# Projecting queries as plain float32 products, and normalising a pair of heads in one product

## The chip, the cores and the metric

One core of a Trainium2 chip runs the whole kernel in one launch. The metric is the device time of an execution in microseconds (us). The kernel before has a median of 1037.31 us over 3 runs (1033.46 to 1041.04).

The engines that matter here: TensorE (PE in the profile, with its weight loads as PEld) does matrix products into PSUM; VectorE (DVE) and ScalarE (ACT) work elementwise on SBUF and PSUM; GpSimd (POOL) works elementwise on SBUF; SyncE (SP) issues all of this kernel's DMAs, one after the other. Each engine executes its instructions in the order in which they were given to it.

## The reference

```python
def phi(x):                                   # x: (4, 8, 576, 64)
    proj = np.einsum('bhsd,df->bhsf', x, w_phi)        # 128 features
    proj = proj - np.max(np.abs(proj), axis=-1, keepdims=True)
    return np.concatenate([np.exp(proj), np.exp(-proj)], axis=-1)
q_p, k_p = (phi(q), phi(k))
kv  = np.einsum('bhsf,bhsd->bhfd', k_p, v)
z   = np.sum(k_p, axis=2)
num = np.einsum('bhsf,bhfd->bhsd', q_p, kv)
den = np.einsum('bhsf,bhf->bhs', q_p, z)[..., None] + 1e-06
x   = (num / den)                             # -> (2304 tokens, 512)
x   = (h * np.cos(h)) @ w_out                 # h = x @ w_in, hidden 2048
out = (np.maximum(h2, 0) + alpha * np.minimum(h2, 0)) @ w_out2   # h2 = x @ w_in2
```

The weights of the two layers arrive as 64-bit floats and are decoded on the chip.

## The kernel before

**Number formats.** TensorE is given two kinds of operand: float32, and float32r, a float32 with a shortened fraction. To keep precision with float32r, a value is split into a high part `hi` (a cast to float32r) and a low part `lo` (the value less `hi`), and a product is made of three: hi·hi, hi·lo, lo·hi. The keys, the queries, `w_phi`, the numerators' operands and both layers are split like this; products of keys' features and values (`kv`) and the transposes of the queries are float32.

**Attention.** The 32 heads are 8 groups of four; a group is two pairs of two heads. The tokens of a group are cut into five chunks: four chunks of two tiles (a tile is 128 rows that hold 128 tokens of both heads of a pair, 256 columns of features), and one chunk of one tile with the last 64 tokens of both pairs. There are 40 chunks of keys and 40 of queries. The loop over `s` (line 710) is the step: in step `s` chunk `s` of the keys is projected and chunk `s - 2` of the queries. The tuple `order` (line 667) lists the stages of a step by hand, and that order is the order on every engine (`tc.manual_schedule()`, line 61).

The queries' way: `load_x` (SP, L358), `split_hi` (DVE cast, L436), `split_lo` (DVE subtraction, L443), `project` (PE, three products per tile, L455) into one of three PSUM buffers `pj` that keys and queries share, `maximum` (DVE, L467), `less_max` (DVE, L475), `q_transpose` (PE, L536), `q_exp` (ACT L555 and L569, then POOL L571 for the low part), `num` (PE, L580), `num_out` (ACT, L593). The keys' way is the same to `less_max`, with the cast on ACT and the subtraction on POOL; then `k_exp` (ACT, L484) and `kv` (PE, L496). Of `kv`, a head's product has 66 columns (64 values, ones, zeros); in the one-tile chunk it has 132.

**Normalising a pair.** When a pair's numerators have left PSUM, `num_out` issues a DMA of the denominators into a tile `dn` (L596). One step later `recip` adds EPS and takes the reciprocal on DVE (L601, L602), writes it to DRAM (L604) and reads it back twice, each head's 576 values broadcast to 64 partitions (L606). One step after that `x_mult` (DVE, L612) multiplies head by head, partitions 0 to 63; the second head's result is written to partitions 64 to 127. Then `x_split` (ACT L621, POOL L623) makes the layers' input `xh`, `xl`.

**Decoding weights.** A part of the weights is ten instructions (`w_instructions`, line 93). Four parts are decoded during the attention, one begun every ten steps (`W_AT`); with `spare=True` DVE does the cast to the high part (L114) and the last subtraction and addition (L132, L133), which in the later parts ACT and POOL do.

**The layers.** From step `S_H` the first products of the layers (L161) run beside the end of the attention, and then alone: 160 steps of hidden product, gate and output product.

Of the kernel before, what the change touches and what calls it, by code (L numbers as in the profile page):

```python
# [23 lines left out]
WARM = 9                    # products that raise the tensor engine's clock  # L24
# [4 lines left out]
def feature_map_attention_two_mlps(  # L29
# [17 lines left out]
    NG4 = qT.shape[0]       # groups of four heads  # L47
# [102 lines left out]
    # ---- the two layers, in steps: a 128-wide part of the hidden dimension for a group of  # L150
    # tokens, and the products that read the part of LEAD steps before
# [91 lines left out]
    # Blocks of parts of the hidden dimension; the first ones are small, so that few weights  # L243
    # have to be on chip when the attention ends. Short group of tokens away from the ends.
# [14 lines left out]
    # A part of the weights is decoded when the last reader of its place has been issued and  # L259
    # before its own first reader is, the rest of the time evenly.  # L260
# [58 lines left out]
    # ---- attention  # L319
    # Group n holds four heads of a batch: two pairs pr of two heads y. A tile has 128 rows  # L320
    # (tokens) for both heads of a pair; the last tile holds the last 64 tokens of both pairs.
    with ExitStack() as actx:
# [23 lines left out]
        xin, xs_h, xs_t, pjs, mxs, tt, kp, kvs = ({} for _ in range(8))  # L346
        q_ps, qp, nm_ps, nums, dens = ({} for _ in range(5))
        kv_todo = []
        rb = (acc[3][0:D, 2 * S:3 * S], acc[4][0:D, 0:S])

        def load_x(kind, i):
            n, c = divmod(i, NC)
            w = len(chunks[c]) * P
            if n == 0:
                return
            t = pool_of[kind].tile([P, 2 * P], F32, tag=f"{kind}in", name=f"{kind}in")
            src = qT if kind == "q" else kT
            nc.sync.dma_start(out=t[:, :w], in_=src[n, :, first[c] * P:first[c] * P + w])  # L358
            xin[kind, i] = t
# [22 lines left out]
        wraw = acc[4][:, S:S + F]  # L382
# [4 lines left out]
        def load_first(kind, c, to):  # L387
            # chunks of the first group, into places that the attention needs later
# [6 lines left out]

        load_first("k", 0, 1)
        for j in range(2):
            nc.sync.dma_start(out=wraw[j * D:(j + 1) * D, :], in_=w_phi)
        load_first("k", 1, 3)
        # the tensor engine's clock is raised while the first inputs arrive  # L400
# [5 lines left out]
        # the exponential's table is loaded while the first inputs arrive  # L406
# [3 lines left out]
        nc.vector.memset(w2h.bitcast(F32), 0.0)  # L410
        nc.vector.memset(w2l.bitcast(F32), 0.0)
# [10 lines left out]
        make_identity(nc, ident)  # L422
        def w_phi_split():
            for j in range(2):
                r = slice(j * D, (j + 1) * D)
                (nc.vector.tensor_copy if j == 0 else nc.scalar.copy)(w2h[r, j, :], wraw[r, :])
                nc.vector.tensor_tensor(
                    out=w2l[r, j, :], in0=wraw[r, :], in1=w2h[r, j, :].bitcast(F32), op=ALU.subtract
                )

        # ---- the stages: i is a chunk, n a group, pr a pair
        def split_hi(kind, i):
            w = len(chunks[i % NC]) * P
            t = xin.pop((kind, i))
            hi = pool_of[kind].tile([P, 2 * P], F32R, tag=f"{kind}h", name=f"{kind}h")
            (nc.scalar.copy if kind == "k" else nc.vector.tensor_copy)(hi[:, :w], t[:, :w])  # L436
            xs_h[kind, i] = (t, hi)

        def split_lo(kind, i):
            w = len(chunks[i % NC]) * P  # L440
            t, hi = xs_h.pop((kind, i))
            lo = pool_of[kind].tile([P, 2 * P], F32R, tag=f"{kind}l", name=f"{kind}l")
            (nc.gpsimd if kind == "k" and i > 1 else nc.vector).tensor_tensor(  # L443
                out=lo[:, :w], in0=t[:, :w], in1=hi[:, :w].bitcast(F32), op=ALU.subtract
            )
            xs_t[kind, i] = (hi, lo)

        def project(kind, i):
            nt = len(chunks[i % NC])
            hi, lo = xs_t.pop((kind, i))  # L450
            pj = ps_pj.tile([P, 2, 2, F], F32, tag="pj", name="pj")
            for a in range(nt):
                s = slice(a * P, (a + 1) * P)
                for m, (l, r) in enumerate(((hi, w2h), (hi, w2l), (lo, w2h))):
                    nc.tensor.matmul(  # L455
                        pj[:, a].rearrange("p j f -> p (j f)"),
                        lhsT=l[:, s],
                        rhs=r.rearrange("p j f -> p (j f)"),
                        start=(m == 0),
                        stop=(m == 2),  # L460
# [78 lines left out]
        def q_exp(i, s, lo):  # L539
# [4 lines left out]
            # columns of tp: tile a, head y (last tile: head y, pair x); parts as (pair, half  # L544
            # of the pair's columns, columns)
# [53 lines left out]
        def recip(n, pr):  # L599
            dn = dens.pop((n, pr))  # L600
            nc.vector.tensor_scalar(out=dn, in0=dn, scalar1=EPS, scalar2=None, op0=ALU.add)  # L601
# [206 lines left out]
```

## Time and profile before

| | |
|---|---|
| runs | 1033.46, 1037.31, 1041.04 us |
| span of the profiled execution, first to last instruction | 1038.0 us (the page gives no other time for it) |
| PE busy | 996.6 us, 96% |
| DVE busy | 755.5 us, 73% |
| ACT busy | 505.3 us, 49% |
| POOL busy | 635.5 us, 61% |
| chain that ended last, by engine | PE 73%, DVE 15%, POOL 4%, issue 3% |
| mean granted TensorE clock | 0.990 of full speed |

A busy share is a mean over the whole span. The attention (about the first 213 us) and the layers (the rest) load the engines differently, so that the shares say little until they are read stretch by stretch. "Busy" is the time in which at least one instruction of an engine was under way. Durations of matmuls in the trace contain their latency; what one costs in a row of them is read from the distance of their starts. Of the rows by line, the number behind the last bar is the idle time of the engine just before such an instruction, with what ended it.

### The profile page before, as it was taken

The numbers are of one execution on the slowest core, as the hardware profiler recorded it, in microseconds if no ns is written. First come the engines' busy times: TensorE is split into PE (matmuls) and PEld (weight loads), VectorE is DVE, ScalarE is ACT, GpSimd is POOL, SyncE is SP. The second block draws the span as 40 slices with busy tenths as digits, with TensorE's granted clock in tenths as the row PEclk, the third lists the DMA queues.
The fourth block names the chain that finished last, engine by engine and source line by source line (L and its number), as shares of the span: only waits on it lengthen the run. The fifth ranks groups of instructions, "written<-read, shape, count | busy, mean of one in ns | idle before, by whom it ended". The sixth has DMA issues, their size and how long they took to land.

```text
span 1038.0 us, 14530 instructions
## 1 busy us (share of the span) xinstructions
PE 996.6 (96%) x5289; PEld 846.4 (82%) x5289; DVE 755.5 (73%) x1090; ACT 505.3 (49%) x1004; POOL 635.5 (61%) x528
## 2 busy tenths in 40 slices
PE   8988888889999999999999999799999999999998
PEld 7888888877888888888888888688888888888887
DVE  6999999976887747765775678567756874777433
ACT  5878777776666556564656573213222231232100
POOL 3878778675666636663657589737564665566411
PEclk8999999999999999999999999999999999999999
DMA  4543433211111101110111011101110111111112
GB/s 119 132 109 96 107 94 96 60 45 51 43 61 46 57 20 42 61 41 22 61 41 41 21 61 41 41 21 62 41 41 23 59 42 40 41 42 41 41 41 102
DMA packets 63303, 58.31 MB, mean 56 GB/s; under 512 B 28672, under 2 KB 54400, under 8 KB 63232
## 3 DMA queue, kind: packets, MB, share of 16 engines
q1 hardware_dynamic: 63232, 57.38, 18.7%
q8 instruction: 42, 0.69, 0.3%
q14 instruction: 29, 0.24, 0.1%
HBM read 52.50 MB, written 4.79 MB: 55 GB/s over the span
## 4 chain that ended last, share of the span: by engine, by line
PE 73%; DVE 15%; POOL 4%; issue 3%; ACT 2%; DMA 1%; SPq 0%; DVEq 0%; POOLq 0%; ACTq 0%
PE po L161 35%; PE ph L161 33%; DVE acc L612 3%; DVE acc L475 3%; PE kv L496 2%; PE nm L580 2%; DVE mx L467 2%; PE pj L455 2%; POOL xl L86 2%; DVE ql L443 1%; DVE we L118 1%; DVE qh L436 1%; DVE wt L122 1%; POOL gl L86 1%; DVE wt L125 1%
## 5 line engine op out<-in xcount | busy, mean ns | idle before, releaser
L86 POOL TENSOR_TENSOR gl<-r,gh 128x512 fp32r<-128x512 f32 (+1 forms) x160 | 201.8, 1263 | 323.7 <-ACT gh L85 314.7
L85 ACT CAST gh<-r 128x512 fp32r<-128x512 f32 (+1 forms) x160 | 92.1, 575 | 387.3 <-DVE r L207 262.1
L161 PE MATMUL ph<-xh,wih 128*128 128x512 f32 (+1 forms) x640 | 237.1, 371 | 2.2 <-DVE kvl L527 2.2
L161 PE MATMUL ph<-xh,wil 128*128 128x512 f32 (+1 forms) x640 | 237.3, 371 | 0.0
L161 PE MATMUL ph<-xl,wih 128*128 128x512 f32 (+1 forms) x640 | 236.5, 370 | 0.0
L236 DVE TENSOR_TENSOR acc<-po,acc 128x512 f32<-128x512 f32 (+1 forms) x134 | 87.0, 659 | 103.8 <-PE po L161 103.3
L161 PEld LDWEIGHTS ph<-xh,wih 128*128 128x128 f32 x640 | 120.8, 189 | 24.5 <-DVE kvl L527 2.5
L161 PEld LDWEIGHTS ph<-xl,wih 128*128 128x128 f32 x640 | 120.8, 189 | 22.3
L161 PEld LDWEIGHTS ph<-xh,wil 128*128 128x128 f32 x640 | 120.9, 189 | 21.4
L161 PE MATMUL po<-gh,woh 128*128 128x512 f32 (+1 forms) x320 | 119.0, 372 | 2.3 <-DVE acc L234 2.3
L161 PE MATMUL po<-wol,gh 128*128 128x512 f32 x288 | 114.8, 399 | 5.3 <-POOL wol L133 5.3
L161 PE MATMUL po<-gh,wol 128*128 128x512 f32 (+1 forms) x320 | 119.6, 374 | 0.1
L161 PE MATMUL po<-gl,woh 128*128 128x512 f32 (+1 forms) x320 | 118.9, 372 | 0.0
L161 PE MATMUL po<-woh,gh 128*128 128x512 f32 x288 | 114.4, 397 | 0.0
L161 PE MATMUL po<-woh,gl 128*128 128x512 f32 x288 | 114.0, 396 | 0.0
L122 DVE SCALAR_TENSOR_TENSOR wt<-ws,we 128x512 int32<-128x512 int32 x64 | 99.8, 1559 | 2.2
L194 DVE TENSOR_SCALAR r<-ph,al 128x512 f32<-128x512 f32 (+1 forms) x80 | 55.3, 691 | 57.3 <-PE ph L161 31.7
L131 POOL TENSOR_TENSOR wu<-wu,we 128x512 f32<-128x512 f32 x64 | 86.0, 1343 | 2.1 <-ACT wu L128 2.1
L571 POOL TENSOR_TENSOR qp1l<-acc,qp1h 128x512 fp32r<-128x512 f32 (+1 forms) x64 | 65.6, 1052 | 28.3 <-ACT qp1h L569 28.1
L205 DVE TENSOR_TENSOR r<-ph,r 128x512 f32<-128x512 f32 (+1 forms) x80 | 50.6, 632 | 43.5 <-ACT r L192 43.4
L496 PE MATMUL kv<-vm,kp 128*128 128x66 f32 x512 | 74.5, 261 | 4.2 <-DVE kvl L527 2.3
L496 PEld LDWEIGHTS kv<-vm,kp 128*128 128x128 f32 x512 | 73.1, 195 | 6.3 <-ACT qp1h L569 2.9
(106 smaller groups left out, 2077.3 us busy)
## 6 DMA issues: line engine op xcount, KB each, us to landing
ws<-in_moe_w_in_dram SPq DMA_DIRECT2D x32, 512.0 KB, 3.7
ws<-in_moe_w_out_dram SPq DMA_DIRECT2D x32, 512.0 KB, 3.5
acc<-dr SPq DMA_DIRECT2D x32, 144.0 KB, 3.3
out_dram<-acc SPq DMA_DIRECT2D x18, 256.0 KB, 2.0
vm<-in_v_dram SPq DMA_DIRECT2D x16, 256.0 KB, 3.6
kin<-in_k_dram SPq DMA_DIRECT2D x28, 128.0 KB, 3.0
qin<-in_q_dram SPq DMA_DIRECT2D x28, 128.0 KB, 2.8
vt<-in_v_dram SPq DMA_DIRECT2D x16, 32.0 KB, 3.4
```

Source lines behind the costliest of these rows:

```text
L85: nc.scalar.copy(hi, src)
L86: lo_engine.tensor_tensor(out=lo, in0=src, in1=hi.bitcast(F32), op=ALU.subtract)
L122: lambda: stt(out=t, in0=w1, scalar=-0x40000000, in1=e, op0=ALU.bitwise_and, op1=ALU.bitwise_or),
L131: lambda: tt(out=u, in0=u, in1=ef, op=ALU.mult),
L161: nc.tensor.matmul(ps, lhsT=l, rhs=r, start=(first and m == 0), stop=(last and m == n - 1))
L194: nc.vector.tensor_scalar(out=r, in0=ph, scalar1=0.0, scalar2=al[:, ft:ft + 1], op0=ALU.min, op1=ALU.mult)
L205: nc.vector.tensor_tensor(out=r, in0=ph, in1=r, op=ALU.mult)
L236: nc.vector.tensor_tensor(out=a, in0=po, in1=a, op=ALU.add)
L475: nc.vector.tensor_tensor(out=t, in0=pj, in1=mx.unsqueeze(2).to_broadcast(list(pj.shape)), op=ALU.subtract)
L496: nc.tensor.matmul(ps[:, :, y, :] if pr is None else ps[:, pr, y, :], lhsT=e[:, s, 2 * a + y, :], rhs=vt[:, y] if pr is None else vm[:, pr ...
L571: nc.gpsimd.tensor_tensor(out=dl, in0=et, in1=dh.bitcast(F32), op=ALU.subtract)
L612: nc.vector.tensor_tensor(out=o[y * D:(y + 1) * D, 0, :], in0=o[0:D, y, :], in1=rb[y], op=ALU.mult)
```

## The change

For the queries `split_hi` and `split_lo` are gone: `project` gives TensorE the loaded float32 tile and a float32 copy `w2` of the weights, one product per tile in place of three. The tile `qin` has four buffers in place of two. `recip` first issues a DMA that copies the second head's numerators from partitions 0 to 63 to partitions 64 to 127, and the broadcasts go to 64 partitions per head of one of two places; `x_mult` is then one multiplication per pair on 128 partitions. The four parts decoded in the attention take `spare=False`. `w2` is cleared before its two DMAs, and `w_phi_split` works on it whole.

```diff
-        rb = (acc[3][0:D, 2 * S:3 * S], acc[4][0:D, 0:S])
+        rb = (acc[3][:, 2 * S:3 * S], acc[4][:, 0:S])
...
-            t = pool_of[kind].tile([P, 2 * P], F32, tag=f"{kind}in", name=f"{kind}in")
+            t = pool_of[kind].tile([P, 2 * P], F32, tag=f"{kind}in", name=f"{kind}in", bufs=4 if kind == "q" else 2)
...
-        wraw = acc[4][:, S:S + F]
+        w2 = const.tile([P, 2, F], F32, name="w2")
...
+        nc.vector.memset(w2, 0.0)
         load_first("k", 0, 1)
         for j in range(2):
-            nc.sync.dma_start(out=wraw[j * D:(j + 1) * D, :], in_=w_phi)
+            nc.sync.dma_start(out=w2[j * D:(j + 1) * D, j, :], in_=w_phi)
...
         def w_phi_split():
-            for j in range(2):
-                r = slice(j * D, (j + 1) * D)
-                (nc.vector.tensor_copy if j == 0 else nc.scalar.copy)(w2h[r, j, :], wraw[r, :])
-                nc.vector.tensor_tensor(
-                    out=w2l[r, j, :], in0=wraw[r, :], in1=w2h[r, j, :].bitcast(F32), op=ALU.subtract
-                )
+            nc.vector.tensor_copy(w2h, w2)
+            nc.vector.tensor_tensor(out=w2l, in0=w2, in1=w2h.bitcast(F32), op=ALU.subtract)
...
         def project(kind, i):
             nt = len(chunks[i % NC])
-            hi, lo = xs_t.pop((kind, i))
+            if kind == "q":
+                x = xin.pop((kind, i))
+                products = ((x, w2),)
+            else:
+                hi, lo = ks_t.pop(i)
+                products = ((hi, w2h), (hi, w2l), (lo, w2h))
...
         def recip(n, pr):
             dn = dens.pop((n, pr))
+            nc.sync.dma_start(out=nums[n, pr][D:2 * D, 0, :], in_=nums[n, pr][0:D, 1, :])
             nc.vector.tensor_scalar(out=dn, in0=dn, scalar1=EPS, scalar2=None, op0=ALU.add)
             nc.vector.reciprocal(dn, dn)
...
                 nc.sync.dma_start(
-                    out=rb[y], in_=dr[y * S:(y + 1) * S].unsqueeze(0).to_broadcast([D, S])
+                    out=rb[pr][y * D:(y + 1) * D, :],
+                    in_=dr[y * S:(y + 1) * S].unsqueeze(0).to_broadcast([D, S]),
                 )
 
-        def x_mult(n, pr, y):
-            o = nums[n, pr]
-            nc.vector.tensor_tensor(
-                out=o[y * D:(y + 1) * D, 0, :], in0=o[0:D, y, :], in1=rb[y], op=ALU.mult
-            )
+        def x_mult(n, pr):
+            x = nums[n, pr][:, 0, :]
+            nc.vector.tensor_tensor(out=x, in0=x, in1=rb[pr], op=ALU.mult)
...
-                w_run.extend(zip((s + d for d in W_PART), w_instructions()))
+                w_run.extend(zip((s + d for d in W_PART), w_instructions(spare=False)))
...
-            chunk(split_hi, 2 - LAG, kind="q"),
...
-            chunk(split_lo, 2 - LAG, kind="q"),
...
-            group(x_mult, after(2), LAG, 0),
-            group(x_mult, after(2), LAG, 1),
+            group(x_mult, after(2), LAG),
```

## Rows read from the trace of the kernel before

**Rows 1.** Windows: stretch in us, its length, each engine's busy time (instructions), granted clock, DMA.

```profile
core 0: us, PE busy (x) PEld busy (x) DVE busy (x) ACT busy (x) POOL busy (x), PEclk, DMA share, GB/s
14.00:213.00 199.00, 174.81 (x1463) 167.28 (x1463) 190.69 (x321) 154.78 (x374) 152.17 (x143) 0.98 0.36 93
67.34:120.48 53.14, 45.29 (x387) 42.91 (x385) 52.09 (x88) 41.59 (x102) 42.50 (x40) 1.00 0.39 101
...
262.00:1038.00 776.00, 766.96 (x3575) 634.42 (x3574) 522.46 (x700) 313.81 (x562) 449.73 (x347) 1.00 0.14 45
```

**Rows 2.** Waits of the engines from 67.34 to 120.48 us: total, times, longest.

```profile
POOL qp1l L571 <- ACT qp1h L569: 7.1, 5, 2.4
...
PE pj L455 <- DVE acc L475: 4.9, 5, 2.5
POOL xl L623 <- ACT xh L621: 4.6, 4, 1.4
...
PE tp L536 <- DVE acc L475: 1.4, 1, 1.4
```

**Rows 3.** Groups by line on DVE, 67.34 to 120.48 us: busy, mean ns, idle before.

```profile
L612 DVE TENSOR_TENSOR acc<-acc,acc 64x576 f32<-64x576 f32 x7 | 9.4, 1339 | 0.1
L443 DVE TENSOR_TENSOR ql<-qin,qh 128x256 fp32r<-128x256 f32 (+1 forms) x10 | 6.7, 672 | 0.0
L436 DVE CAST qh<-qin 128x256 fp32r<-128x256 f32 (+1 forms) x10 | 5.3, 530 | 0.0
...
L133 DVE TENSOR_TENSOR wil<-wt,wu 128x512 fp32r<-128x512 f32 x1 | 1.0, 1035 | 0.1
L114 DVE CAST wih<-wt 128x512 fp32r<-128x512 f32 x1 | 1.0, 961 | 0.0
...
L132 DVE TENSOR_TENSOR wt<-wt,wih 128x512 f32<-128x512 f32 x1 | 0.8, 837 | 0.0
```

**Rows 4.** The line of x_mult: duration ns min/median/max, first and last start.

```profile
L612 DVE TENSOR_TENSOR acc<-acc,acc x27: 737/905/1822, 50.9 to 237.8; 64x576 f32<-64x576 f32 x27
```

**Rows 5.** Timeline of PE, 60 to 90 us: start, us, instruction, how many in a row.

```profile
69.07 0.39 PE L580 MATMUL nm<-qp1l,kvh 128*66 128x320 f32 x1
69.30 0.39 PE L496 MATMUL kv<-vt,kp 128*128 128x132 f32 x2
69.44 0.39 PE L580 MATMUL nm<-qp1h,kvl 128*66 128x320 f32 x1
...
70.40 0.31 PE L580 MATMUL nm<-qp1h,kvl 128*66 128x320 f32 x1
70.55 0.30 PE L580 MATMUL nm<-qp1h,kvh 128*66 128x320 f32 x1
...
72.56 0.28 PE L455 MATMUL pj<-w2h,qh 128*128 128x256 f32 x1
...
72.91 0.28 PE L455 MATMUL pj<-w2h,qh 128*128 128x256 f32 x1
...
73.27 1.90 PE L496 MATMUL kv<-vm,kp 128*128 128x66 f32 x16
75.00 0.39 PE L536 MATMUL tp<-ident,acc 128*128 128x128 f32 x2
```

**Rows 6.** Decoding of the later parts: duration ns min/median/max, first and last start.

```profile
L114 ACT CAST wih<-wt x30: 613/616/622, 245.5 to 920.6; 128x512 fp32r<-128x512 f32 x30
L132 POOL TENSOR_TENSOR wt<-wt,wih x30: 1287/1305/1486, 248.2 to 923.3; 128x512 f32<-128x512 f32 x30
L133 POOL TENSOR_TENSOR wil<-wt,wu x30: 1276/1298/1623, 249.6 to 924.6; 128x512 fp32r<-128x512 f32 x30
```

**Rows 7.** Timeline of DVE, 79 to 89 us: one pair's reciprocal and products.

```profile
79.54 0.16 DVE L601 TENSOR_SCALAR dn<-dn 128x9 f32<-128x9 f32 x1
...
86.61 2.50 DVE L612 TENSOR_TENSOR acc<-acc,acc 64x576 f32<-64x576 f32 x2
```

**Rows 8.** Timeline of SP, 79 to 83 us: the same pair's DMAs.

```profile
79.98 0.33 SPq L604 DMA_DIRECT2D dr<-dn  x1
81.40 1.09 SPq L606 DMA_DIRECT2D acc<-dr  x2
```

**Rows 9.** Page, DMA issues: line, count, KB each, median us from issue to landing.

```profile
acc<-dr SPq DMA_DIRECT2D x32, 144.0 KB, 3.3
```

**Rows 10.** Timeline of PE, 216 to 219 us: where the layers begin, idle before in brackets.

```profile
218.22 0.65 PE L161 MATMUL ph<-xh,wih 128*128 128x512 f32 x1 [2.22 <-DVE kvl L527]
```

More of the change, by code (lines that the diff above doesn't have):

```diff
@@ L345, in feature_map_attention_two_mlps @@
         pool_of = {"q": wk, "k": kw}
-        xin, xs_h, xs_t, pjs, mxs, tt, kp, kvs = ({} for _ in range(8))
+        xin, ks_h, ks_t, pjs, mxs, tt, kp, kvs = ({} for _ in range(8))
         q_ps, qp, nm_ps, nums, dens = ({} for _ in range(5))
         kv_todo = []
-        rb = (acc[3][0:D, 2 * S:3 * S], acc[4][0:D, 0:S])
+        rb = (acc[3][:, 2 * S:3 * S], acc[4][:, 0:S])
         def load_x(kind, i):
@@ L409, in feature_map_attention_two_mlps @@
         nc.vector.memset(half_pi, math.pi / 2)
-        nc.vector.memset(w2h.bitcast(F32), 0.0)
-        nc.vector.memset(w2l.bitcast(F32), 0.0)
         for vm, vt in vbuf:
@@ L423, in w_phi_split @@
         def w_phi_split():
-            for j in range(2):
-                r = slice(j * D, (j + 1) * D)
-                (nc.vector.tensor_copy if j == 0 else nc.scalar.copy)(w2h[r, j, :], wraw[r, :])
-                nc.vector.tensor_tensor(
-                    out=w2l[r, j, :], in0=wraw[r, :], in1=w2h[r, j, :].bitcast(F32), op=ALU.subtract
-                )
-        def split_hi(kind, i):
-            w = len(chunks[i % NC]) * P
[L434 to L437, printed above, removed]
@@ L439, in split_lo, with split_hi @@
-        def split_lo(kind, i):
+            nc.vector.tensor_copy(w2h, w2)
+            nc.vector.tensor_tensor(out=w2l, in0=w2, in1=w2h.bitcast(F32), op=ALU.subtract)
+        def split_hi(i):
+            w = len(chunks[i % NC]) * P
+            t = xin.pop(("k", i))
+            hi = kw.tile([P, 2 * P], F32R, tag="kh", name="kh")
+            nc.scalar.copy(hi[:, :w], t[:, :w])
+            ks_h[i] = (t, hi)
+        def split_lo(i):
             w = len(chunks[i % NC]) * P
-            t, hi = xs_h.pop((kind, i))
-            lo = pool_of[kind].tile([P, 2 * P], F32R, tag=f"{kind}l", name=f"{kind}l")
-            (nc.gpsimd if kind == "k" and i > 1 else nc.vector).tensor_tensor(
+            t, hi = ks_h.pop(i)
+            lo = kw.tile([P, 2 * P], F32R, tag="kl", name="kl")
+            (nc.gpsimd if i > 1 else nc.vector).tensor_tensor(
@@ L444, in split_lo @@
                 out=lo[:, :w], in0=t[:, :w], in1=hi[:, :w].bitcast(F32), op=ALU.subtract
             )
-            xs_t[kind, i] = (hi, lo)
+            ks_t[i] = (hi, lo)
         def project(kind, i):
             nt = len(chunks[i % NC])
-            hi, lo = xs_t.pop((kind, i))
+            if kind == "q":
[4 more added lines that the diff above has]
+                products = ((hi, w2h), (hi, w2l), (lo, w2h))
@@ L451, in project @@
             pj = ps_pj.tile([P, 2, 2, F], F32, tag="pj", name="pj")
             for a in range(nt):
-                s = slice(a * P, (a + 1) * P)
-                for m, (l, r) in enumerate(((hi, w2h), (hi, w2l), (lo, w2h))):
+                for m, (l, r) in enumerate(products):
                     nc.tensor.matmul(
                         pj[:, a].rearrange("p j f -> p (j f)"),
-                        lhsT=l[:, s],
+                        lhsT=l[:, a * P:(a + 1) * P],
                         rhs=r.rearrange("p j f -> p (j f)"),
@@ L459, in project @@
                         start=(m == 0),
-                        stop=(m == 2),
+                        stop=(m == len(products) - 1),
                     )
@@ L654, in go @@
                 i = s + d
-                if 0 <= i < NK and not (f == split_hi and kind == "k" and i < 2):
+                if 0 <= i < NK and not (f == split_hi and i < 2):
                     f(*(() if kind is None else (kind,)), i, *a)
@@ L676, in feature_map_attention_two_mlps @@
             chunk(q_exp, -LAG - 2, 1, False),
-            chunk(split_hi, 2, kind="k"),
+            chunk(split_hi, 2),
             chunk(q_exp, -LAG - 2, 1, True),
@@ L687, in feature_map_attention_two_mlps @@
             group(num, NUM_AT, LAG),
-            chunk(split_lo, 2, kind="k"),
+            chunk(split_lo, 2),
             chunk(maximum, -LAG, kind="q"),
             lambda s: kv_some(),
-            chunk(split_lo, 2 - LAG, kind="q"),
             chunk(q_transpose, -LAG - 1),
             group(kv_lo, KV_AT, 0),
-            group(x_mult, after(2), LAG, 0),
-            group(x_mult, after(2), LAG, 1),
+            group(x_mult, after(2), LAG),
             chunk(less_max, -LAG, kind="q"),
@@ L704, in feature_map_attention_two_mlps @@
         assert S_H < S_O < S_H + LEAD_H
-        split_hi("k", 0)
-        split_lo("k", 0)
+        split_hi(0)
+        split_lo(0)
         w_phi_split()
-        split_hi("k", 1)
-        split_lo("k", 1)
+        split_hi(1)
+        split_lo(1)
         for s in range(NS):
```

## The prediction

> **What bounds the kernel now.** I read the windows first, then who waits for whom, and only then the single groups. The windows [rows 1] show two kernels in one. After 262 us TensorE is busy 767.0 of 776 us: the layers are bound by its products, none of which the change touches, so I carry these 776 us over unchanged. In the attention, 14 to 213 us, the engine that hardly rests is VectorE: 190.7 of 199 us, against 174.8 on TensorE, 154.8 on ScalarE and 152.2 on GpSimd.
>
> The order of stages repeats every ten steps (two groups of heads, one decoded part of the weights). I take one such stretch as a ledger, 67.34 to 120.48 us, 53.14 us long: VectorE 52.1, TensorE 45.3, GpSimd 42.5, ScalarE 41.6 [rows 1]. The waits in it say the same [rows 2]: TensorE's largest are for VectorE's `less_max` (4.9 and 1.4 us of its 53.14 - 45.29 = 7.9 idle). GpSimd's, 7.1 and 4.6 us, are for ScalarE. So VectorE sets the pace, but the others have only 8 to 12 us of room per stretch: relief on VectorE can be worth that much at most, whatever is taken from it. 199 / 53.14 = 3.7 such stretches lie in the attention.
>
> **What leaves VectorE, per stretch.** The queries' splits: 6.7 + 5.3 = 12.0 us [rows 3]. The decoding's cast, subtraction and addition: 1.0 + 0.8 + 1.0 = 2.8 us [rows 3]. Of eight multiplications of a head, four remain, one per pair; seven of them cost 9.4 us, 1.34 each [rows 3], so about 5.4 us go. One multiplication took between 0.74 and 1.82 us [rows 4]; the new one has the same 576 columns on twice the partitions, both ends stand for it too (2.9 to 7.3 us per stretch), and I take the mean. Together 20.2 us: VectorE would have about 32 us of work in a stretch, far from the bound. It is not the gain.
>
> **What is added.** TensorE: a query tile costs three products now, 72.91 - 72.56 = 0.35 us [rows 5]. A float32 product shows as two instructions (the `kv` rows). Nearest to the new one, with more columns than a weight load hides behind, is the 132-column `kv`: from one `nm` to the next with two of them between takes 69.44 - 69.07 = 0.37 us, an `nm` alone 70.55 - 70.40 = 0.15, so the two take 0.22, and for 256 columns I take 0.22 x 256/132 = 0.43 us. That is 0.08 more per tile, and 18 tiles in a stretch make 1.5 us. The bounds: two instructions at the pace of the split ones, 2 x 0.35/3 = 0.23, would save 2.2 us per stretch; at the pace of the 66-column `kv`, sixteen in 75.00 - 73.27 = 1.73 us, thus 0.108 per 66 columns, it is 0.84 us a tile, and 8.8 us more per stretch. I stay at the 132-column row, since the 66-column ones follow each other at a pace that their columns don't explain (half the columns, the same 0.11 us).
>
> The Trainium skill (FP8 and Floating Point Precision, TensorE Precision Notes) counts a true float32 product as four passes through the array, against the three split products here. By that rule a tile would cost a third more than 0.35 us, which is an estimate of 0.47, and the stretch 2.1 us in place of 1.5; the total would come out 2 us later than mine. The `kv` row puts it a little under four, and I keep to the row.
>
> GpSimd gets the subtraction and the addition of a decoded part, 1.31 + 1.30 = 2.6 us per stretch, ScalarE the cast, 0.62 us [rows 6]: GpSimd 45.1, ScalarE 42.2.
>
> The second head's copy: one DMA per pair, ahead of `dr` in SyncE's order. Its issue costs about half of the 1.09 us that two broadcasts take there [rows 8], its landing I put at that of the 144 KB broadcast, 3.3 us [rows 9]; the ends are nothing (it flies while the reciprocal goes out and comes back) and its whole 3.3 us in the pair's chain. The multiplication stands in front of the query's `less_max` on VectorE, so if it waits, the transposes of the next step wait. In the pair at 79.54 us the reciprocal begins there, the second broadcast is issued at about 81.95 and should have landed at 85.2, and the multiplication begins at 86.61 [rows 7 to 9]: 1.4 us to spare. With the queries' splits gone VectorE could come there up to 2.4 us earlier (12.0 us over ten steps, two of them between reciprocal and multiplication), and the copy adds about 0.5. So the multiplication will now wait 1 to 1.5 us per pair, 4 to 6 us per stretch, out of the 16 us that VectorE has to spare in a stretch of 48. I cost it at nothing; without that cover 1.5 us at each of 16 pairs would be 24 us. The four `qin` buffers, the one clearing of `w2` and its two whole-width splits replace work of the same few instructions at the start: nothing.
>
> **The sum.** Per stretch TensorE has 45.3 + 1.5 = 46.8 us. Of its 7.9 us of waits the 6.3 us for `less_max` should go and 1.6 stay (those for ScalarE's features among them): 48.4 us, against GpSimd's 45.1 and ScalarE's 42.2. That is 4.7 us less than 53.14, and 3.7 x 4.7 = 17.5 us. Where the layers begin, TensorE waits 2.2 us for `kvl` [rows 10], which is queued on VectorE behind the last decoded part's addition; that addition goes to GpSimd, and I count the 2.2. Together 19.7 us: 1038.0 - 19.7 = 1018.3 for the profiled execution, which stands 0.7 above the median of the runs, so 1017.6. **I predict 1018 us**: the attention is then bound by TensorE, with GpSimd and ScalarE close behind it.
>
> The forecast's own range: if TensorE's waits go altogether and GpSimd loses some of what it now waits in VectorE's company, a stretch of 45.5 gives 3.7 x 7.6 + 2.2 = 30 us, thus about 1007; if they go by half, 3.7 x 2 + 2.2, it is 1028.
>
> **Rivals.**
>
> *GpSimd's chain takes over.* For: it gets the added 2.6 us, its steps are uneven, and 11.7 us of its idle time are waits for ScalarE [rows 2], which itself waits for others. If of these only the 4.6 us behind the normalised pair go, a stretch is 45.1 + 7.1 = 52.2 us, and 3.7 x 0.9 + 2.2 gives 6 us: 1031. Against: part of ScalarE's lateness comes from VectorE and goes with it.
>
> *The multiplication's wait holds VectorE (slower).* Place: `x_mult`, behind reciprocal, copy and broadcasts, all on SyncE, whose loads of the keys stand between. With 32 us of work and w us of wait per pair, VectorE needs 32 + 4w us per stretch: the whole gain is gone at w = 5.3, and at w = 6.5 a stretch is 58 us: 3.7 x 4.9 - 2.2 = 16 us longer, 1053. Against: the chain is 6 to 7 us in all, and the two steps between take 9.6 us at the forecast's pace, so that w stays near 1.
>
> *The float32 products run at the 66-column pace.* Then TensorE has 45.3 + 8.8 = 54.1 us per stretch, and with its 1.6 us of other waits 55.7: 3.7 x 1.0 - 2.2 to 3.7 x 2.6 - 2.2 us longer, 1039 to 1045. Against: the 132-column row. Small.
>
> **How the numbers follow.** About 1%, 10 us, is what a measurement of this kernel can tell from no change. The forecast has 0.72, GpSimd's chain 0.20, the slower wait 0.04, the slow products 0.04. Faster by over 1% (under 1027) is nearly all of the forecast and a fifth of GpSimd's case: 0.74. Within 1%: the rest of GpSimd's case, the slow end of the forecast and half of the slow products: 0.21. Slower: 0.05. The range runs from 1005, just under the forecast's best, to 1032, which takes in GpSimd's 1031.
>
> **What would show it.** After the change, the windows should have VectorE at 60 to 75% of the attention and TensorE above 93%; the rows of `qh` and `ql` are gone; a query tile on TensorE shows two instructions with starts about 0.22 us apart; TensorE's waits for `less_max` are small; the layers' stretch is still some 776 us long, and the attention ends some 20 us earlier. It would be wrong if GpSimd has no gaps and the others wait for it, if `x_mult` waits over 4 us per pair, or if the layers' stretch changes.

## The result, and the profile after

The kernel after takes 1011.44 us (median of 4 runs, 1010.16 to 1013.05); the kernel before, run beside it, 1036.38 us. The ratio is 0.9751, with a 95% interval of 0.9721 to 0.9781: 2.5% faster. The forecast was 1018 us, in a range of 1005 to 1032. The direction and the mechanism came out as predicted, the gain was larger than its sum, one wait that the sum took as free was not, and a part of the gain came from the start, for which the sum had no term.

The windows of the kernel after, core 0: the attention, ten steps of it, and the layers.

```profile
core 0: us, PE busy (x) PEld busy (x) DVE busy (x) ACT busy (x) POOL busy (x), PEclk, DMA share, GB/s
11.00:188.00 177.00, 172.39 (x1406) 163.95 (x1404) 133.99 (x226) 156.47 (x382) 149.56 (x151) 1.00 0.45 118
62.40:108.00 45.60, 44.78 (x370) 42.71 (x368) 34.05 (x59) 41.34 (x102) 40.94 (x41) 1.00 0.50 129
...
236.00:1008.40 772.40, 762.69 (x3557) 630.98 (x3555) 518.52 (x695) 311.46 (x557) 448.71 (x346) 1.00 0.13 45
```

Read the second row against its twin in [rows 1]. Ten steps went from 53.14 to 45.60 us. The next ten took 46.52 us, where they had taken 53.37. VectorE fell from 52.09 to 34.05 us, out of the way; TensorE has 44.78 of 45.60, and ScalarE and GpSimd lie 3.4 and 3.8 us under it. In the layers TensorE is as dense as before (762.7 of 772.4 us; before 767.0 of 776.0).

So the time came out of the attention. The layers' first product starts at 188.84 us, where it started at 218.22 [rows 10]: 29.4 us earlier. From there to the first output product of the layers it takes 1.6 us less (the granted clock from 220 to 240 us was 0.95 before and is 1.00 after), and the rest to the end 1.4 us more. The spans differ by 1038.0 - 1008.4 = 29.6 us, the medians by 24.9. The runs after are about 1.8 us longer than their spans (1010.16 for the 1008.4 here), so the profiled execution of before was a long one among the few runs of that kernel taken here: some 2.5 to 3.4 us above their median, not the 0.7 that the prediction took from setting the span itself against the median. Beside the experiments below the kernel before had medians of 1038.7 to 1039.4 us, over 7 to 13 runs each; by those the profiled execution was an ordinary one, and 24.9 us is a low figure for the gain.

Not all of the 29.4 us come from the repeated steps. This is TensorE at the start, before (with the window from 10 to 20 us, and the first key product of step 10):

```profile
9.76 0.35 PE L455 MATMUL pj<-w2h,qh 128*128 128x256 f32 x1 [2.02 <-DVE qh L436]
...
11.11 3.51 PE L496 MATMUL kv<-vm,kp 128*128 128x66 f32 x16
...
18.80 0.60 PE L536 MATMUL tp<-ident,acc 128*128 128x128 f32 x4
...
44.18 0.36 PE L455 MATMUL pj<-w2h,kh 128*128 128x256 f32 x1
```

```profile
10.00:20.00 10.00, 10.00 (x61) 9.90 (x61) 7.40 (x17) 2.75 (x8) 1.47 (x2) 0.66 0.49 101
```

and after:

```profile
8.63 1.10 PE L455 MATMUL pj<-w,acc 128*128 128x256 f32 x4 [0.55 <-DMA acc<-in_q_dram]
9.57 1.90 PE L496 MATMUL kv<-vm,kp 128*128 128x66 f32 x16
...
14.65 0.61 PE L536 MATMUL tp<-ident,acc 128*128 128x128 f32 x4
...
39.91 0.36 PE L455 MATMUL pj<-w2h,kh 128*128 128x256 f32 x1
```

```profile
10.00:20.00 10.00, 9.89 (x80) 9.43 (x78) 7.57 (x13) 6.48 (x16) 4.43 (x5) 1.00 0.47 97
```

Before, TensorE waits 2.02 us for VectorE's cast of the first query. Behind this wait the granted clock of TensorE is 0.66 of full speed, so that it stood at the lower of its two levels (1.2 and 2.4 GHz) for most of the window, and sixteen `kv` products take 3.51 us. After, no cast stands before the first query's product; the wait is 0.55 us, the clock stays at 1.00, and the same sixteen products take 1.90 us. The first transposes start 4.15 us earlier, and at step 10 the lead is 4.3 us, hardly more. The other 25.1 us come behind it. In the profiles of the experiments below the window from 10 to 20 us has 0.66 wherever all queries are split, as before, and 1.00 in all others but one (0.50). A wait of that length does not always bring the fall: the queries' part with four key buffers waits 2.0 us there and has 1.00. There is one profile of each kernel, so how often the clock falls is not shown.

The waits of the kernel after from 11 to 188 us (engine, line waited at, releaser: total, times, longest) name no `less_max` on TensorE any more [rows 2]. VectorE waits instead, for the broadcasts of the normalisation. TensorE's 2.3 us at its transposes (`tp`) are put down to `dn`, which they do not read; `less_max`, whose result they do read, is the instruction just before it on VectorE:

```profile
DVE acc L615 <- DMA acc<-dr: 11.4, 7, 3.6
...
ACT kh L432 <- DMA kin<-in_k_dram: 7.5, 5, 2.8
...
DVE dn L603 <- DMA dn<-acc: 7.3, 3, 3.1
...
PE tp L536 <- DVE dn L603: 2.3, 3, 1.1
...
PE pj L455 <- PE pj L455: 2.1, 4, 0.7
```

The timeline of TensorE after (start, duration, instruction, how many in a row) shows the new projection: four instructions for two query tiles, 64.04 - 63.18 = 0.86 us, so 0.43 us a tile, against 0.35 for three split products [rows 5]. The trace names `w2` as `w`.

```profile
62.40 0.37 PE L455 MATMUL pj<-w2h,kh 128*128 128x256 f32 x1
...
63.18 1.02 PE L455 MATMUL pj<-w,qin 128*128 128x256 f32 x4
64.04 1.90 PE L496 MATMUL kv<-vm,kp 128*128 128x66 f32 x16
```

The groups by line of after, 62.4 to 108 us (instructions, busy us, mean ns, idle before and what ended it):

```profile
L615 DVE TENSOR_TENSOR acc<-acc,acc 128x576 f32<-128x576 f32 x3 | 2.3, 755 | 3.1 <-DMA acc<-dr 3.1
...
L571 POOL TENSOR_TENSOR qp1l<-acc,qp1h 128x512 fp32r<-128x512 f32 (+1 forms) x16 | 14.4, 928 | 2.0 <-ACT qp1h L569 2.0
L571 POOL TENSOR_TENSOR qp0l<-acc,qp0h 128x512 fp32r<-128x512 f32 x8 | 10.6, 1348 | 0.3 <-ACT qp0h L569 0.2
...
L439 POOL TENSOR_TENSOR kl<-kin,kh 128x256 fp32r<-128x256 f32 (+1 forms) x10 | 6.8, 680 | 0.0
```

The same GpSimd groups of before, 67.34 to 120.48 us:

```profile
L571 POOL TENSOR_TENSOR qp1l<-acc,qp1h 128x512 fp32r<-128x512 f32 (+1 forms) x16 | 16.3, 1041 | 7.1 <-ACT qp1h L569 7.1
L571 POOL TENSOR_TENSOR qp0l<-acc,qp0h 128x512 fp32r<-128x512 f32 x8 | 11.3, 1425 | 0.3 <-ACT qp0h L569 0.2
...
L443 POOL TENSOR_TENSOR kl<-kin,kh 128x256 fp32r<-128x256 f32 (+1 forms) x10 | 8.0, 805 | 0.0
```

GpSimd does the same instructions in less time: 1041 to 928, 1425 to 1348 and 805 to 680 ns, together 3.8 us a stretch. The subtraction and addition that it took over cost it 3.1 us there.

### The profile page after: what moved, and what is told of

Its sections match the earlier page's. It is cut to its first block, busy times and chain, and to the rows that moved or that the text cites. A ratio compares the mean times of both kernels' runs of the same rounds, so it can differ in the third digit from the quotient of the medians.

```text
span 1008.4 us, 14301 instructions
## 1 busy us (share of the span) xinstructions
PE 988.7 (98%) x5217; PEld 838.6 (83%) x5217; DVE 687.5 (68%) x980; ACT 504.7 (50%) x1007; POOL 630.7 (63%) x536
## 3 DMA queue, kind: packets, MB, share of 16 engines
q1 hardware_dynamic: 64512, 59.75, 19.7%
## 4 chain that ended last, share of the span: by engine, by line
PE 81%; DVE 6%; DMA 5%; POOL 4%; ACT 3%; issue 1%; SPq 1%; DVEq 0%; POOLq 0%; ACTq 0%
PE po L161 36%; PE ph L161 33%; PE pj L455 4%; PE kv L496 4%; PE nm L580 3%; DMA acc<-dr 2%; POOL xl L86 2%; DMA dn<-acc 1%; PE tp L536 1%; DMA dr<-dn 1%; DVE wt L122 1%; POOL gl L86 1%; DVE wt L125 1%; DVE we L118 0%; DVE acc L475 0%
## 5 line engine op out<-in xcount | busy, mean ns | idle before, releaser
L496 PE MATMUL kv<-vm,kp 128*128 128x66 f32 x512 | 72.2, 255 | 0.1
L125 DVE SCALAR_TENSOR_TENSOR wt<-wu,wt 128x512 f32<-128x512 f32 x64 | 68.0, 1062 | 5.5 <-ACT wu L117 1.6
```

Source lines behind the costliest of these rows:

```text
L125: lambda: stt(out=tf, in0=u, scalar=MIN_PATTERN, in1=tf, op0=ALU.is_ge, op1=ALU.mult),
L496: nc.tensor.matmul(ps[:, :, y, :] if pr is None else ps[:, pr, y, :], lhsT=e[:, s, 2 * a + y, :], rhs=vt[:, y] if pr is None else vm[:, pr ...
```

## Experiments: which part brings the gain

All medians below are of 4 to 10 runs, each ratio is against the kernel before, run beside it. Adding the change by thirds to the kernel before comes first.

**The queries alone**, on the kernel before: unsplit queries with four buffers, `w2`, no splits.

```diff
+            if kind == "q":
+                products = ((xin.pop((kind, i)), w2),)
...
-            chunk(split_hi, 2 - LAG, kind="q"),
...
-            chunk(split_lo, 2 - LAG, kind="q"),
```

> The kernel before with the first part alone: queries as one float32 product per tile, four query buffers. Theory A (ceiling): in a stretch of ten steps the attention lasts as long as the larger of VectorE's and TensorE's work. VectorE falls from 52.1 to about 41 us, TensorE is at 45 to 46, so the stretch is 46 to 47.5 us and the kernel takes 1012 to 1017 us: this part alone brings nearly the whole gain of 25. Theory B (shares): each part brings time in proportion to what it takes from VectorE, 12.0 of 20.2 us: 15 us, 1021 us.

Measured: 1012.57 us, ratio 0.9751 (0.9723 to 0.9779). Its ten steps, in the window:

```profile
67.44:113.63 46.19, 45.14 (x370) 42.82 (x368) 42.42 (x67) 41.20 (x101) 42.23 (x40) 1.00 0.46 121
```

This part alone has the whole gain of the change, that of the start included. VectorE still has 42.4 us of 46.2, but TensorE has 45.1: with VectorE 2.7 us under it, taking more from VectorE does not show, as long as the keys have two buffers (the experiments with four are below).

**The pair alone**, and **the decoding alone**, each on the kernel before:

```diff
+            nc.sync.dma_start(out=nums[n, pr][D:2 * D, 0, :], in_=nums[n, pr][0:D, 1, :])
...
+            x = nums[n, pr][:, 0, :]
+            nc.vector.tensor_tensor(out=x, in0=x, in1=rb[pr], op=ALU.mult)
```

> The kernel before with the second part alone: the second head's copy by DMA and one multiplication per pair. Theory A (ceiling): VectorE falls from 52.1 to about 47 us and still bounds, the stretch is 47 to 49 us, the kernel takes 1017 to 1024 us. Theory B (shares): 5.4 of 20.2 us, 7 us: 1030 us. If the wait for copy and broadcasts counts while VectorE is the bound, it is less than B gives, 1033 us or more.

```diff
-                w_run.extend(zip((s + d for d in W_PART), w_instructions()))
+                w_run.extend(zip((s + d for d in W_PART), w_instructions(spare=False)))
```

> The kernel before with the third part alone: cast, subtraction and addition of the four decoded parts on ScalarE and GpSimd. Theory A (ceiling): VectorE falls from 52.1 to about 49.5 us, 3.7 x 2.6 = 10 us and up to 2 at the start of the layers: 1025 to 1029 us. Theory B (shares): 2.8 of 20.2 us, 3.5 us: 1033 us.

**Both of them without the queries' part:**

> The kernel before with the second and third parts, the queries still split on VectorE and projected with three products. Theory A (ceiling): VectorE has about 44 to 46 us in a stretch, TensorE 1.5 less than in the changed kernel, thus 43.3; the two are level and the kernel takes 1009 to 1016 us, as the changed one within a few us. Theory B (shares): 8.2 of 20.2 us, 10 us: 1026 us.

Measured: the pair 1023.16 us, 0.9851 (0.9820 to 0.9882); the decoding 1034.34 us, 0.9958 (0.9939 to 0.9978); both 1022.48 us, 0.9843 (0.9813 to 0.9873). Their windows of ten steps, in that order, one fence for each kernel:

```profile
73.25:120.74 47.49, 44.49 (x387) 42.93 (x386) 45.77 (x84) 41.47 (x101) 41.76 (x40) 1.00 0.49 126
```

```profile
73.81:125.92 52.11, 46.22 (x388) 44.27 (x386) 50.89 (x86) 42.14 (x102) 45.27 (x42) 0.97 0.41 104
```

```profile
48.20:96.17 47.97, 44.48 (x388) 42.97 (x386) 45.84 (x82) 41.97 (x101) 43.86 (x43) 1.00 0.47 125
```

The pair gives 1.5%, as theory A expected. The decoding gives 0.4%, 5.1 us by the medians, where theory A expected 10 to 12, and nothing on top of the pair: my expectation of 1009 to 1016 us for both was missed. In all three VectorE is still at 96 to 98% of the stretch.

VectorE's groups by line from 20 to 200 us, with the pair alone and with both, show where the decoding's relief went. With the pair alone the cast, the subtraction and the addition take 11.4 us there. With both they are gone, but the queries' casts take 719 ns in the mean in place of 569 and their subtractions 761 in place of 675, together 8.3 us more, while GpSimd has 156.2 us of work in place of 151.2. The parts do not add: 2.5, 1.5 and 0.4% alone, 2.5% together.

## Experiments: what bounds the kernel after

**Keys unsplit too.** Every projection is a float32 product, and keys and queries have four buffers each.

```diff
-            if kind == "q":
-                x = xin.pop((kind, i))
-                products = ((x, w2),)
-            else:
-                hi, lo = ks_t.pop(i)
-                products = ((hi, w2h), (hi, w2l), (lo, w2h))
+            x = xin.pop((kind, i))
+            products = ((x, w2),)
...
-            chunk(split_hi, 2),
...
-            chunk(split_lo, 2),
```

> The changed kernel with the keys projected as one float32 product too: the keys' cast leaves ScalarE, their subtraction leaves GpSimd (some 8 us of its 41 per stretch), TensorE gets 0.08 us more per tile. Theory A (TensorE is the bound after the change): 72 tiles x 0.08 = 6 us slower than the changed kernel, 1016 to 1018 us. Theory C (GpSimd's or ScalarE's chain is the bound after the change): as fast or faster, 1005 to 1011 us.

**Four buffers for the keys** (and three for the queries, for space), nothing else:

```diff
-... bufs=4 if kind == "q" else 2)
+... bufs=3 if kind == "q" else 4)
```

> The changed kernel with four buffers for loaded keys and three for loaded queries in place of two and four, so that SyncE is not held by the keys' loads ahead of a pair's copy and reciprocal. Theory A: x_mult waits less (23 us in all in the changed kernel) and TensorE's last 4.6 us of idle time between 11 and 188 us shrink: 1 to 4 us faster, 1007 to 1011 us. If the pair's wait is covered in any case: no difference.

**Some queries split again**, in two of five chunks, on VectorE, to use its idle time and spare TensorE 0.08 us a tile (with three query buffers in place of four, for space):

```diff
+        Q_SPLIT = (1, 3)
...
+            if kind == "q" and i in qs_t:
+                hi, lo = qs_t.pop(i)
+                products = ((hi, w2h), (hi, w2l), (lo, w2h))
```

> The changed kernel with two of five chunks of the queries (32 of 72 tiles) split on VectorE again and projected with three products. Theory A (TensorE bounds, VectorE has room): TensorE gets 32 x 0.08 = 2.6 us less, 2 to 3 us faster, 1008 to 1010 us. Theory C, or VectorE's order of work already in the way: the same or slower, 1011 to 1016 us.

**A key product less**: the product of the keys' high part and the weights' low part is left out, so TensorE has 72 x 0.35/3 = 8.4 us less work in the attention.

```diff
-                products = ((hi, w2h), (hi, w2l), (lo, w2h))
+                products = ((hi, w2h), (lo, w2h))
```

> The changed kernel without the second of the keys' three products (high part by the weights' low part), all else as it is: 72 x 0.118 = 8.5 us less on TensorE, nothing less on any other engine. Theory A (TensorE bounds): 6 to 8.5 us faster, 1003 to 1006 us, since ScalarE and GpSimd have 41 us of work in a stretch of 46. Theory C (their chain bounds): 1009 to 1012 us.

These four ran beside each other. Measured: keys unsplit 1011.24 us, 0.9740 (0.9719 to 0.9760); key buffers 1006.44 us, 0.9695 (0.9673 to 0.9717); some queries split 1012.77 us, 0.9756 (0.9735 to 0.9778); a key product less 1014.17 us, 0.9768 (0.9744 to 0.9792). Windows of the first (attention), the second (ten steps) and the last (50 us):

```profile
11.00:185.00 174.00, 173.91 (x1326) 163.72 (x1325) 135.27 (x226) 146.38 (x343) 123.72 (x114) 1.00 0.47 121
```

```profile
62.83:107.08 44.25, 44.25 (x370) 42.68 (x368) 35.24 (x61) 41.39 (x103) 41.72 (x42) 1.00 0.51 134
```

```profile
60.00:110.00 50.00, 44.83 (x360) 42.12 (x359) 37.44 (x66) 44.06 (x108) 43.05 (x44) 1.00 0.46 120
```

The last row refutes the simple form of my theory, that TensorE's work alone sets the pace of the kernel after. Less work on TensorE gave no time back; it became idle time (5.2 of 50 us), and the kernel was slower than either theory had expected. Something else held the attention at the same length. Splitting some queries again gave nothing back either, where theory A expected 2 to 3 us.

The second row says what was free to take. With more buffers for the keys TensorE is busy in every microsecond of the stretch, and the kernel is 5.0 us faster than the one after by the medians; the intervals, 0.9673 to 0.9717 and 0.9721 to 0.9781, do not touch. The kernel after did not run beside it, but two kernels with two key buffers did, at 1012.8 and 1014.2 us. No other kernel of this study has a lower median; it is faster than before and after.

Keys unsplit is no slower than the kernel after, where theory A expected 6 us. But it has the buffers too, and so has to be compared with the kernel that has them: it is 4.8 us slower, with TensorE at 173.91 of 174 us. 72 tiles at the measured 0.08 us more are 5.8 us. Where TensorE is really full, a float32 product costs what its pace says.

**Both at once, and the changed parts again with the buffers.** First the buffers with the key product left out:

> The kernel with four key buffers (1006 us) without the second of the keys' three products: 8.5 us less on TensorE, nothing less elsewhere. Theory D (the changed kernel was held by two limits that lay level, TensorE's work and the keys' loads with two buffers; with four buffers TensorE alone is left): 5 to 8 us faster than with four buffers, 998 to 1002 us, where the same cut brought nothing with two. Theory C (ScalarE's or GpSimd's chain is the bound in any case): 1005 to 1009 us.

Then the buffers with some queries split again (the queries loaded into free columns of `acc`, for space):

> The kernel with four key buffers, and two of five chunks of the queries split on VectorE and projected with three products (the loaded queries stand in four free places of the accumulators). Theory D: TensorE gets 32 x 0.08 = 2.6 us less and VectorE has room: 1003 to 1005 us. Theory C: 1006 to 1009 us.

Then the buffers with the queries' part alone, so without the pair's and the decoding's:

> The kernel before with unsplit queries and four key buffers alone, without the pair's single multiplication and with the decoding's share left on VectorE. Theory D: VectorE has some 41 us of work in a stretch that TensorE fills with 45, so these two parts bring nothing here either: 1005 to 1009 us. If VectorE's relief by them counts once the loads are out of the way: 1010 to 1014 us.

Measured: 1007.88 us, 0.9704 (0.9665 to 0.9743); 1007.28 us, 0.9704 (0.9680 to 0.9729); 1011.51 us, 0.9746 (0.9719 to 0.9772). Windows of the first (the start, and ten steps) and of the third (50 us):

```profile
0.00:25.00 25.00, 21.62 (x92) 18.00 (x93) 12.14 (x25) 10.18 (x23) 7.08 (x21) 0.73 0.66 156
107.39:150.99 43.60, 42.87 (x352) 40.78 (x350) 34.87 (x60) 41.53 (x102) 42.25 (x43) 1.00 0.51 133
```

```profile
60.00:110.00 50.00, 49.05 (x397) 46.53 (x397) 46.73 (x74) 45.54 (x111) 46.27 (x44) 1.00 0.42 109
```

The first was expected at 998 to 1002 us and missed that. Its runs fall in two groups, 1003.57 and 1004.07, and 1011.69 and 1011.78; the profiled one had a granted clock of 0.73 in its first 25 us (TensorE had waited 1.8 us for the first query), where the kernel after had 1.00, so its median is not a fair price. The ten steps are one: 43.60 us, only 0.65 less than with the buffers alone, although TensorE has 1.4 us less to do. GpSimd is now at 42.25 (97%) and ScalarE at 41.53, and GpSimd's low parts of the queries (`qp0l`, `qp1l`) make up 8.0% of the chain of work from 60 to 160 us, where with the buffers alone only TensorE stands in it. They lie so close under TensorE that cutting TensorE further is worth less than 1 us in this stretch. The second, sparing TensorE by a detour over VectorE, gains nothing over the buffers, and theory D's 1003 to 1005 us were missed. Its chain from 60 to 160 us has other things in it: `less_max` with 7.5%, the loads of the queries into `acc` with 7.4%, the broadcasts with 6.6%. So the detour itself is not priced by it.

The third shows what the pair's and the decoding's parts are good for. The buffers bring the queries' part alone nothing to speak of (1012.57 and 1011.51 us; theory D expected 1005 to 1009). With all parts they bring 5 us. VectorE's 93% of the window is not the reason by itself: the second kernel has 47.43 us of the same 50 on VectorE (95%) and takes 1007.28 us. The chain of the third from 60 to 160 us says more:

```profile
by line: PE pj L454 29.6%; PE kv L495 26.7%; PE nm L579 24.4%; PE tp L535 8.9%; DVE acc L611 4.8%; DVE acc L474 2.2%; issue 1.7%; DVE mx L466 1.2%; DVE kvl L526 0.7%
```

The queries' part with two buffers has the same chain to 0.1 points. No DMA stands in either. What does is VectorE's multiplication head by head (L611) with 4.8%, and `less_max` behind it (L474). In the kernel after the multiplication is down to 0.8%, but the transfers of the normalisation have 25.7% (shown below). As I read it, one multiplication per pair saves with two key buffers about what it loses in waiting, and with four it only saves. Whether the decoding's part is needed for that was not tried.

**What may hold the 5 us: the order on SyncE.** SyncE's timeline of the kernel after (issue start, us, instruction):

```profile
107.20 0.33 SPq L358 DMA_DIRECT2D kin<-in_k_dram  x1
...
108.10 0.52 SPq L602 DMA_DIRECT2D acc<-acc  x1
108.71 0.54 SPq L606 DMA_DIRECT2D dr<-dn  x1
111.78 1.10 SPq L608 DMA_DIRECT2D acc<-dr  x2
```

and VectorE's over the same pair, with its idle time before an instruction in brackets, and then TensorE's:

```profile
105.88 0.64 DVE L603 TENSOR_SCALAR dn<-dn 128x9 f32<-128x9 f32 x1 [3.07 <-DMA dn<-acc]
106.55 0.22 DVE L604 RECIPROCAL dn<-dn 128x9 f32<-128x9 f32 x1
...
115.68 0.76 DVE L615 TENSOR_TENSOR acc<-acc,acc 128x576 f32<-128x576 f32 x1 [3.23 <-DMA acc<-dr]
116.36 0.68 DVE L475 TENSOR_TENSOR acc<-pj,mx 128x512 f32<-128x512 f32 x1
```

```profile
117.19 0.63 PE L536 MATMUL tp<-ident,acc 128*128 128x128 f32 x4 [1.07 <-DVE dn L603]
```

Follow one pair. The reciprocal is ready at 106.77 us. `dr` could go then, but SyncE stands at the load of `kin`, whose buffer GpSimd has not freed; it goes at 107.20, a load of `qin` and the pair's copy behind it, and `dr` at 108.71. The broadcasts go at 111.78, the multiplication begins at 115.68 after 3.23 us of waiting, `less_max` sits behind it, and TensorE, which wants its result, idles 1.07 us. So I left the buffers as the change has them and moved the copy and `dr` ahead of the step's loads:

```diff
-            group(recip, after(1), LAG),
+            group(spread, after(1), LAG),
...
+            group(recip, after(1), LAG)(s)
```

(`recip` now ends with `dr`; the stage `spread` has the two broadcasts and stands where `recip` stood.)

> The changed kernel, buffers as in it, with another order on SyncE alone: a pair's copy and the write of the reciprocals are issued ahead of the step's loads, the two broadcasts stay behind them. Theory E (what four key buffers gave back was the time in which SyncE, held by a key load that waits for its buffer, could not issue the pair's DMAs): the multiplication waits less and most of the 5 us comes back, 1006 to 1009 us. Theory F (the keys' loads themselves came too late with two buffers): no gain or a loss, since the loads now stand behind the reciprocal, 1011 to 1016 us.

Measured: 1008.17 us, 0.9705 (0.9681 to 0.9729). The waits of SyncE for a key buffer, 11 to 185 us, in the kernel after, with the key buffers, and with the order alone:

```profile
SPq L358 <- POOL kl L439: 38.7, 21, 5.4
```

```profile
SPq L358 <- PE pj L455: 32.6, 19, 4.8
...
SPq L358 <- POOL kl L439: 4.7, 8, 1.8
```

```profile
SPq L358 <- POOL kl L439: 18.2, 12, 5.4
```

The key buffers do not free SyncE: with three buffers for the queries it then stands 32.6 us at loads that wait for TensorE's projection. But it is through with them when the reciprocal comes. From the end of the reciprocal to the issue of `dr` it takes 1.2 to 2.1 us in five of the 16 pairs of the kernel after, and 0.1 us or less in the others; with the key buffers 1.1 us once and 0.2 or less otherwise; with the order 0.03 in every pair. In the kernel before it was 0.3 or less in all of them.

The chain of work from 60 to 160 us by line, of the same three:

```profile
by line: PE pj L455 20.6%; PE nm L580 19.1%; PE kv L496 18.8%; DMA acc<-dr 10.0%; DMA dr<-dn 8.1%; DMA dn<-acc 7.6%; PE tp L536 6.1%; DVE acc L475 4.3%; issue 2.9%; DVE mx L467 2.7%; DVE dn L603 1.4%; SPq L608 1.4%; DVE acc L615 0.8%; DVE d
```

```profile
by line: PE pj L455 31.7%; PE kv L496 30.7%; PE nm L580 28.7%; PE tp L536 9.0%
```

```profile
by line: PE pj L455 27.3%; PE kv L496 25.4%; PE nm L580 24.1%; PE tp L536 7.4%; DMA acc<-dr 4.3%; DMA dn<-acc 3.2%; DMA dr<-dn 2.6%; issue 2.1%; POOL wol L133 1.4%; SPq L358 0.7%; POOL kl L439 0.7%; DVE dn L603 0.5%; SPq L614 0.5%; DVE dn L
```

In the kernel after, the three transfers of the normalisation are 25.7% of the chain; with the order 10.1%, with the buffers none. The multiplication's waits fall in the same way: 11.4 us, then 5.6, then 2.0. And so do those of TensorE behind it (`tp`, put down to `dn`: 2.3, then 0.3, then none). The order alone takes off 3.3 us by the medians; its interval touches that of the kernel after by 0.0008, so its size is less sure than that of the buffers. What it does to the chain is plain.

## Why the prediction was right, step by step

**VectorE sets the pace before, and TensorE after.** Right for the repeated steps. The queries' part alone shows it: VectorE 42.4, TensorE 45.1 of 46.2 us, and the whole gain is there. VectorE's own work was forecast at 32 us a stretch and is 34.05.

**The float32 product costs 0.43 us a tile, 1.5 us a stretch.** Right, and to the digit; the 132-column row was the fitting neighbour. Keys unsplit priced it a second time: 4.8 us for 72 tiles. The Trainium skill (FP8 and Floating Point Precision, TensorE Precision Notes) counts four passes, which made 0.47 us; the trace has 0.43, 1.23 times the split product where that rule has 1.33.

**A stretch of 48.4 us: a mis-sized term.** The prediction put TensorE's own work at 45.3 + 1.5 = 46.8 us, and 1.6 us of waits on top. The trace has 44.78 and 0.82. With the key buffers TensorE never rests, and the whole stretch with the new products is 44.25 us; without their 1.5 that leaves some 42.7 us of real work in the stretch of before, where the window said 45.3. The other 2.6 us of its "busy" were, most likely, the latency of products that end in front of a wait: a split product shows as 0.28 us while the next starts 0.12 us later [rows 5], and TensorE stops ten times in that stretch. So a stalled engine's busy time is no sum of work. That made the gain per stretch 7.5 us where the sum had 4.7. It is the forecast's best case (45.5 us), by a route that the prediction had named only in part.

**3.7 stretches, and nothing at the start.** 3.7 x 7.5 + 2.2 = 30.1 us comes near the 29.4 us by which the layers begin earlier, but by luck. Up to step 10 the steps gained 0.1 us, and behind it 25.1, the 2.2 us at the layers among them: 3.7 stretches were too many. The 4.2 us of the start fill the gap, and the prediction has no term for them. It read the attention from 14 us on, and names no wait of TensorE before that.

**GpSimd at 45.1 us.** Too high: 40.94. Its added work came (3.1 us for the two instructions), but 3.8 us went from the groups shown above, and the stretch of before held one `xl` more (five against four, 1.0 us). The rival in which it takes over did not occur at this pace; it is the next bound, though, as the cut key product showed.

**The copy and the multiplication's wait, costed at nothing.** The place was right, the price was not nothing. The wait was forecast at 1 to 1.5 us per pair, under cover of VectorE's spare time. It came in 7 of the 13 pairs multiplied before 188 us, 11.4 us in all, up to 3.6 us at once; over a wait that long the cover gave way, since `less_max` stands behind it and TensorE behind that. What it cost is at most what the order (3.3 us) and the buffers (5.0 us) gave back. The cause, key loads that hold SyncE in front of the copy and `dr`, was named in the rival of the slower wait; that one's price (over 5.3 us per pair) was far from reached. Two of the last three pairs, behind 188 us, did wait 4.4 and 4.9 us, over the 4 us that the prediction had set as a sign against it. The layers' products run beside them by then, and with the key buffers the same two waits are 5.2 and 4.9 us in a faster kernel.

**The wait of 2.2 us where the layers begin** is gone, as forecast. **The layers unchanged**: from their first output product to the end, 798.5 us before and 799.9 after. **The slow float32 products**: false.

**From span to median.** The span fell by 29.6 us where the sum had 19.7. The median fell by 24.9, since the profiled execution was slower than the median of the four runs before and, at 1010.16 us, 1.3 us faster than the median after. So 1018 was 6.6 us too high, not 10. Of the 9.9 us by which the span was missed, the start is 4.2.

What stays open: how much of the buffers' 5 us is the multiplication and how much the keys themselves, which ScalarE waited for (`kh`, 7.5 us in the kernel after, 0.4 with the buffers); the order alone left 2.5 us of TensorE's waits at `pj`, which the buffers took to 0.2. The profile puts these down to TensorE itself, so their true releaser isn't shown. Nor was it tried whether order and buffers together give more, or which of the pair's and the decoding's parts the buffers need.

## What to carry to other kernels

Read the stalled engine's work from a stretch in which it never waits, or from distances of starts in full rows; its busy share in a stalled stretch contains the latency of the products before each wait. Read the start by itself: what a change does to the first wait, and to the clock behind it, is no share of a repeated stretch. When relief on the bounding engine passes the next engine, further relief buys nothing by itself: find the next wait, here a queue. On an engine that issues DMAs in order, ask of each issue what stands ahead of it that can wait for a buffer, and put the short, late-needed chain first or give the waiting load more buffers.

## What the runs showed of the hardware

**Twice the partitions, the same time.** The product of 576 columns takes 743 to 760 ns on 128 partitions where nothing disturbs it, and took 737 on 64 [rows 4]. The line of it in the kernel after (ns min/median/max, first and last start):

```profile
L615 DVE TENSOR_TENSOR acc<-acc,acc x14: 743/760/1890, 44.4 to 207.8; 128x576 f32<-128x576 f32 x14
```

Three of the stretch's four multiplications have a mean of 755 ns, at the lower of the two ends that the prediction put for it; the fourth took 1026.

**VectorE and GpSimd hold each other up.** Where the multiplication takes over 0.78 us, seven times of 16, GpSimd was at work when it started. VectorE and then GpSimd in the kernel after, for one of them:

```profile
53.09 1.66 DVE L615 TENSOR_TENSOR acc<-acc,acc 128x576 f32<-128x576 f32 x1
```

```profile
52.84 1.29 POOL L132 TENSOR_TENSOR wt<-wt,wih 128x512 f32<-128x512 f32 x1
54.21 1.67 POOL L133 TENSOR_TENSOR wil<-wt,wu 128x512 fp32r<-128x512 f32 x1
```

The multiplication starts 0.25 us after GpSimd's instruction and ends 0.62 us after its end, which is nearly its undisturbed 0.75; GpSimd's next, begun before that, takes 1.67 us where it took 1.28 to 1.30 [rows 6]. The Trainium skill (SBUF — State Buffer, SBUF: two separate sides) says that a VectorE operation with two SBUF inputs and a GpSimd operation that reads SBUF take a port pair as an exclusive lock, for the whole instruction; these rows agree with it. It is a likely reason, too, why GpSimd's groups above became shorter when the queries' subtractions left VectorE, but no run here shows which instruction had held them.

**A float32 projection is two instructions that start 0.215 us apart** (four in 0.86 us, 256 columns), so twice the columns of the 132-column product of [rows 5] cost about twice as much.
